# A planned attention and softplus MLP kernel: another block order, single ranks, a quartered end

## The chip, the core and the metric

The kernel runs on one core of a Trainium2 chip. The metric is the device time of one execution in microseconds; lower is better. An execution is followed by its engines: TensorE (PE), VectorE (DVE), ScalarE (ACT), GpSimd (POOL), and SyncE (SP), which issues all the DMAs.

## What is computed

The reference is an attention with a compressive memory, followed by a two-layer perceptron with softplus. The two weight matrices arrive as 64-bit words.

```python
B, H, S, D = 4, 8, 576, 64
scores = causal(q @ k.T / sqrt(D))
local = softmax(scores) @ v
q_p = elu(q) + 1
mem_out = (q_p @ M_prev) / (q_p @ z_prev + 1e-6)
x = sigmoid(beta) * mem_out + (1 - sigmoid(beta)) * local      # 2304 tokens x 512
out = softplus(x @ w_in) @ w_out                               # w_in 512 x 2048, w_out 2048 x 512
```

## The kernel before

**Blocks.** Each of the four batches is cut into two windows of queries, A (256 tokens) and B (320), so there are eight token blocks, numbered 0 to 7: even ones are A (narrow), odd ones B (wide). A batch has four pairs of heads (16 units of V in all), and a pair in a window is a "half", 0 to 31. The 2048 hidden columns are 16 groups f of 128.

**Three kinds of work.** (1) Attention: for each half `memory`, `chunks`, `values` make 128 rows of x and write them, as a high and a low part, to `xhl` and to DRAM (`xd`). (2) Fill: when the four halves of a block are done, `fill` multiplies x by the groups f = 0 to 6 (`hin`, then products into `part` in DRAM). Their weights are decoded at the start from 64-bit words (`decode`: load, one step on POOL or ACT, three on DVE, then a high and a low half; the low half of the pairs in `PELO` is made by two PE matmuls and an ACT copy, that of the others by a POOL subtraction). (3) Tail: `rest`, for each block in `ORDER`, reloads x, scales it (`halved`, with a square on ACT at L1011, a POOL clamp, a PE sum and small DVE steps), runs the groups f = 7 to 15 in float16 high and low parts, and adds `part`. Their weights come from `second`: load into a ring of two buffers (`ws` for w_in, `ws2` for w_out), decode, a square on ACT (L522), POOL clamp (L503), PE sum (L493), scale on DVE, then the two halves on ACT and DVE. `group` needs the scales of all 18 weights, and the g of every tail block (`parts16`, L1120 and L1122) needs `group`. `OPT['zp']` says which of these weights (number 2f + i, i = 1 for w_out) have their first step on ACT (L363) and not on POOL (L359).

**Plain and halved blocks.** A tail block in `SEVEN` computes x @ w_in for pairs of groups with seven products of half the columns in place of eight (`seven`, L1170; `combos` makes sums of the weights, on POOL for the pairs in `OPT['sp']`, their low halves on POOL for `OPT['sl']`; `halved` adds x's parts at L1015, on POOL for blocks in `OPT['zx']`). The other two blocks are `plain` (L394). The out-products are L1285; they collect in PSUM, and at a block's end DVE adds `part` (L1297) and SP sends the output (L1299).

**What sets the order.** Every operation is put on record by `op(engine, duration, rank, fn, reads, writes, dma=...)`. `Plan.run` then goes through time with these durations and gives each engine, of the operations that could start within 60 ns of the earliest, the one with the lowest rank. The order that results is fixed per engine: the engine's queue runs in that order, and an operation that waits holds all behind it. Ranks come from tables: `DEC` for `decode`, `SLOT` and `RK` for attention, `DT` for `second`, `XT` and `RKT` for the tail. A DMA's landing is reckoned as 1.4 us, its `dma` time behind the queue, and 0.7 us. Where PE is expected to idle in the first 130 us, filler matmuls (L1383) are put in. At the start 40 matmuls (L1375) run as warm-up.

**Buffers.** `xhl` has two buffers, used in the order of the calls: fill 6 and fill 7 hold them last in attention, the first tail block takes that of fill 6. The pools of the late weights and of the tail (`wl`, `wr`) open when attention's pools are released. For halves under `PHS` the feature map of `memory` stays in two parts and PE sums them (L911); for the others POOL adds them first (L903).

**V's scale.** `v_prep` finds a power of two for V of a unit. For units in `OPT['ab']` it is DVE's absolute maximum (L855); for the others two ACT passes of Relu (L847) with an added sum (L860).

**The end.** In `rest` each group's out-product has two parts of two 128-row quarters, and each part has its eviction and its output DMA. The last block is number 2, narrow.

Of the kernel before, what the change touches and what calls it, by code (L numbers as in the profile page):

```python
# [13 lines left out]
BF16 = mybir.dt.bfloat16  # L14
# [17 lines left out]
ORDER = [7, 0, 3, 4, 5, 1, 6, 2]  # L32
SEVEN = {1, 2, 3, 4, 5, 6}
CAP = 320
DEC = {(0, 0): -482.398, (1, 0): 24.68, (2, 0): -334.061, (3, 0): -530.087, (4, 0): -67.263, (5, 0): -115.974, (6, 0): 76.265, (0, 1): -777.236, (1, 1): 776.884, (2, 1): 980.305, (3, 1): 576.745, (4, 1): 532.208, (5, 1): -1374.13, (6, 1): -320.298}
PELO = {(0, 1), (4, 0), (2, 1), (1, 1), (2, 0), (5, 1), (3, 0), (1, 0), (4, 1)}
PHS = 12
RK = {'v': -14.703, 'mem': 77.969, 'prod': 27.412, 'norm': 41.42, 'r': -75.809, 'hi': -54.159, 'lo': 49.423, 'vhi': -231.603, 'vlo': 9.162, 'val': -74.716, 'qz': -35.724}
SLOT = {0: -523.489, 3: 179.471, 20: -126.975, 2: -551.32, 24: -61.418, 8: -436.367, 17: -51.528, 13: -174.167, 12: -191.109, 5: -136.439, 27: -23.647, 9: 273.018, 6: 31.405, 23: -191.858, 26: -120.491, 29: 70.495, 22: -62.923, 16: -216.806, 10: -1.497, 21: 29.964, 14: -303.101, 4: -317.571, 15: -59.449, 28: -418.019, 7: -98.43, 19: 320.22, 25: -47.394, 1: 14.992, 11: -79.481, 18: 247.429, 30: 186.958, 31: 184.083}
# [60 lines left out]
class Plan:  # L100
# [182 lines left out]
def attn_softplus_moe(  # L283
# [559 lines left out]
    def v_prep(u, k):  # L843
        va, vb, sc = u.va, u.vb, u.sc

        def acc(j):
            A.activation(out=vb()[:, 0].bitcast(BF16), in_=va(), func=AF.Relu, scale=1.0 - 2.0 * j,  # L847
                         accum_out=sc()[:, 3 + j:4 + j])

        def total():  # L850
            return sc()[:, 5:6].bitcast(BF16)[:, 0:1]

        sp = R["sm"].new()
        if u.no in OPT["ab"]:
# [14 lines left out]
        def scale():  # L869
            si = sc().bitcast(I32)  # L870
            V.tensor_scalar(out=si[:, 0:1], in0=sp().bitcast(I32)[:, 0:1], scalar1=0x7F800000, scalar2=None,
                            op0=ALU.bitwise_and)
            V.tensor_scalar(out=si[:, 1:2], in0=si[:, 0:1], scalar1=-1.0, scalar2=float(261 << 23), op0=ALU.mult,
                            op1=ALU.add)

        op("DVE", 340, k, scale, r=[sp], w=[(sc, 1)])
# [376 lines left out]
    LAG = 3  # L1253

    def rest(bi):
# [4 lines left out]
        for t in range(2):  # L1260
            op("SP", 450, 0, lambda t=t: SY.dma_start(out=xh()[:, t, :, :n], in_=xd[:, t, :, t0:t0 + n]),
               r=[(X[bi], p) for p in range(4)], w=[(xh, 4 * t + p) for p in range(4)], dma=5.8 * n)
# [4 lines left out]
           r=[(PART[bi], dm) for dm in range(4)], w=[(pp, e) for e in range(2)], dma=5.8 * n)  # L1267
# [8 lines left out]
        fs = [f for f in FINE]  # L1276
        for pair in PAIRS:
# [12 lines left out]
        for e in range(2):  # L1290
# [150 lines left out]
```

## Time and profile before

| | |
|---|---|
| time, median of 3 executions | 592.14 us (591.72 to 594.23) |
| the profiled execution | 597.28 us, of which span 595.5 us |
| granted clock of TensorE, mean | 0.993 of 2.4 GHz |
| PE busy | 567.5 us |
| DVE busy | 445.3 us |
| ACT busy | 376.1 us |
| POOL busy | 179.1 us |
| DMA | 90.11 MB, mean 151 GB/s |
| filler matmuls L1383 | 10.3 us of PE's busy time |

The span runs from the first to the last instruction; the profiled execution's own time is 1.8 us longer. Busy time of PE counts filler and warm-up too. Waits are put down to the instruction that released them, which may itself have waited; they have to be followed back.

### The profile page before, as it was taken

What the parts mean: (1) busy time and instruction counts of PE and PEld (TensorE: products, weight loads), DVE (VectorE), ACT (ScalarE), POOL (GpSimd) and SP (SyncE); (2) the same over time, 40 slices, a digit from 0 to 9 for tenths busy, and PEclk for the clock granted to TensorE, in tenths of its full rate; (3) what the DMA queues carried; (4) which work ended last, traced back from release to release, by engine and by line L of the source; (5) the groups of instructions that cost most, each with busy time, mean ns of one, the idle gap of its engine ahead of it and who ended that gap; (6) DMA issues with size and microseconds to landing.
All of it is one profiled execution on the core that took longest, in us unless ns stands there. A gap on an engine that the chain in (4) does not pass through costs nothing. (4 is left out here: it accounts for less than half of the span.)

```text
span 595.5 us, 14222 instructions
## 1 busy us (share of the span) xinstructions
PE 567.5 (95%) x5412; PEld 475.2 (80%) x5412; DVE 445.3 (75%) x1027; ACT 376.1 (63%) x1007; POOL 179.1 (30%) x265
## 2 busy tenths in 40 slices
PE   6989999899999999999999979989999999999996
PEld 5666667787887888788879979856888898888996
DVE  6698788888878789889885759979776566665643
ACT  6656766656566675777563657765565566565653
POOL 3664432545437334445541100003600101000100
PEclk9999999999999999999999979999999999999999
DMA  8654458997899899999969753940231432221111
GB/s 305 211 175 138 166 157 211 202 204 163 181 215 197 203 175 190 199 140 203 175 139 195 257 177 127 309 147 0 90 126 36 140 110 80 72 81 36 47 36 36
DMA packets 131027, 90.11 MB, mean 151 GB/s; under 512 B 85904, under 2 KB 122768, under 8 KB 130960
## 3 DMA queue, kind: packets, MB, share of 16 engines
q1 hardware_dynamic: 130960, 89.22, 59.7%
q8 instruction: 42, 0.69, 0.5%
q14 instruction: 25, 0.20, 0.1%
HBM read 49.84 MB, written 18.87 MB: 115 GB/s over the span
## 5 line engine op out<-in xcount | busy, mean ns | idle before, releaser
L1285 PE MATMUL s<-g,y 128*128 128x320 f16 (+1 forms) x864 | 120.4, 286 | 1.2 <-ACT g L1120 0.8
L394 PE MATMUL h<-xhl,w 128*128 128x256 f32 (+1 forms) x672 | 102.4, 301 | 1.4 <-ACT gl L1221 1.1
L394 PE MATMUL h<-g,w 128*128 128x256 f32 (+1 forms) x672 | 101.7, 303 | 0.8 <-ACT gl L1221 0.3
L1285 PEld LDWEIGHTS <-y 128*128 128x128 f16 x864 | 81.7, 98 | 19.4 <-issue 1.7
L394 PEld LDWEIGHTS h<-xhl,w 128*128 128x128 f32 x672 | 91.8, 189 | 6.2 <-issue 1.9
L394 PEld LDWEIGHTS h<-g,w 128*128 128x128 f32 x672 | 92.6, 192 | 4.5 <-issue 2.0
L729 POOL TENSOR_SCALAR PHL<-P,rr 128x384 f16<-128x384 f32 (+3 forms) x100 | 62.7, 642 | 75.5 <-DVE rr L709 28.4
L679 ACT ACTIVATE P<-s,nm 128x128 f32<-128x128 f32 (+3 forms) x128 | 66.5, 526 | 3.7 <-DVE rr L707 0.9
L1122 DVE SCALAR_TENSOR_TENSOR g<-gq,iv,g 128x320 f16<-128x320 f32 (+1 forms) x72 | 41.1, 581 | 28.4 <-ACT g L1120 28.2
L733 DVE SCALAR_TENSOR_TENSOR PHL<-P,rr,PHL 128x384 f16<-128x384 f32 (+3 forms) x100 | 58.5, 608 | 0.2 <-POOL PHL L729 0.2
L668 DVE TENSOR_REDUCE nm<-s 128x2 f32<-128x768 f32 (+2 forms) x64 | 51.0, 816 | 9.3 <-PE s L662 9.1
L1120 ACT ACTIVATE g<-gq,iv 128x320 f16<-128x320 f32 (+1 forms) x72 | 37.5, 531 | 5.1 <-PE s L1285 2.2
L1170 PEld LDWEIGHTS <-w 128*128 128x128 f16 x576 | 39.1, 98 | 1.8 <-issue 0.3
L1187 ACT ACTIVATE gq<-gq,iv 128x320 f32<-128x320 f32 (+3 forms) x48 | 21.6, 468 | 29.7 <-DVE gq L1182 29.6
L394 PE MATMUL h<-x,v 128*128 128x320 f16 (+1 forms) x288 | 38.1, 286 | 2.0 <-ACT gq L1139 1.4
L1221 ACT ACTIVATE gl<-h 128x256 f32<-128x256 f32 (+1 forms) x56 | 22.8, 409 | 27.0 <-PE h L394 26.8
L503 POOL TENSOR_SCALAR xs<-xs 128x1 bf16<-128x1 f32 x8 | 6.8, 847 | 98.5 <-ACT x L1011 98.5
L394 PEld LDWEIGHTS <-v 128*128 128x128 f16 x288 | 27.8, 98 | 10.2 <-issue 3.3
L957 PEld LDWEIGHTS <-vb 128*64 128x64 f16 x508 | 25.3, 109 | 11.5 <-issue 7.2
L327 DVE TENSOR_TENSOR g<-gl,g 128x256 fp32r<-128x256 f32 (+1 forms) x56 | 28.0, 506 | 8.5 <-ACT g L333 7.5
L1170 PEld LDWEIGHTS <-v 128*128 128x128 f16 x432 | 30.3, 98 | 2.4
L674 ACT ACTIVATE nm<-nm 128x2 f32<-128x2 f32 (+2 forms) x64 | 12.9, 202 | 27.3 <-DVE nm L668 24.6
(190 smaller groups left out, 1094.0 us busy)
## 6 DMA issues: line engine op xcount, KB each, us to landing
ws<-in_w_in_dram SPq DMA_DIRECT2D x16, 512.0 KB, 4.5
ws<-in_w_out_dram SPq DMA_DIRECT2D x16, 512.0 KB, 4.3
va<-in_nat_dram SPq DMA_DIRECT2D x16, 320.0 KB, 4.8
xd<-xhl SPq DMA_DIRECT2D x16, 320.0 KB, 3.3
xhl<-xd SPq DMA_DIRECT2D x8, 640.0 KB, 6.4
kB<-in_nat_dram SPq DMA_DIRECT2D x16, 288.0 KB, 3.9
xd<-xhl SPq DMA_DIRECT2D x16, 256.0 KB, 3.1
xhl<-xd SPq DMA_DIRECT2D x8, 512.0 KB, 4.8
```

The costliest lines, as they stand in the source:

```text
L327: eng.tensor_tensor(out=out, in0=in0, in1=in1, op=ALU.subtract)
L394: MM(out, lhsT=l, rhs=r, start=start and i == 0, stop=stop and i == len(pairs) - 1)
L668: V.tensor_reduce(out=nm()[:, 2 * j * both:2 * j * both + 2], in_=s()[:, :, so[j]:so[j] + n], op=ALU.max, axis=AX.X, negate=True)
L679: A.activation(out=pt()[:, po[j] + h * n:po[j] + h * n + n], in_=s()[:, h, so[j]:so[j] + n], func=AF.Softplus, scale=SCALE, bias=nm()[:, o ...
L729: P.tensor_scalar(out=o[:, :, 0, h, :], in0=src, scalar1=rs, scalar2=0.0, op0=ALU.mult, op1=ALU.add)
L733: V.scalar_tensor_tensor(out=o[:, :, 1, h, :], in0=src, scalar=rs, in1=o[:, :, 0, h, :], op0=ALU.mult, op1=ALU.subtract)
L957: MM(out, lhsT=vb()[:, vi, kc, 64 * h:64 * h + 64], rhs=rhs, start=False, stop=(kc == kcs[-1] and i == len(combos) - 1), skip_group_check= ...
L1120: op("ACT", 200 + .833 * n, -1, lambda: A.activation(out=g()[:, 0, :n], in_=gl(), func=AF.Copy, scale=sc()), r=gr + [(iv, 1)], w=[(g, 0)])
L1122: op("DVE", 165 + 1.04 * n, -1, lambda: V.scalar_tensor_tensor(out=g()[:, 1, :n], in0=gl(), scalar=sc(), in1=g()[:, 0, :n], op0=ALU.mult, ...
L1170: MM(bank()[:, :m], lhsT=left(s, kd, u), rhs=right(q, kd, v), start=first and not kd and not z, stop=kd == 1 and z == 2, skip_group_check= ...
L1221: op("ACT", 170 + .833 * n, -1, lambda: A.activation(out=gl()[:, :n], in_=hp()[:, :n], func=AF.Softplus, scale=XSC), r=[hp], w=[gl])
L1285: MM(bank(dm), lhsT=l, rhs=r, start=f == fs[0] and q == 0 and (not small or dm % 2 == 0), stop=f == fs[-1] and q == 2, skip_group_check=True)
```

## The change

Eight things change together. `ORDER` begins with block 3 (now the plain wide one) and puts block 7, attention's last, fifth; `SEVEN` follows. A table `NUDGE` adds a rank to 243 single operations, counted in the order of the `op` calls. The tables of ranks and of engines get other values (`PELO` loses (4, 0) and (1, 0); `PHS` goes from 12 to 11). For units not in `OPT['ab']` (3 before, 3 and 9 after) the sum of squares of one ACT pass takes the place of the two Relu passes. The load of x in the tail is reckoned at 7.0 n in place of 5.8 n. The last block's out-product has three parts, quarters (0, 1), (2,) and (3,), each with its eviction and DMA, and the last one's rank is `END` = 3 later. From `NUDGE` the entries are left out.

```diff
-ORDER = [7, 0, 3, 4, 5, 1, 6, 2]
-SEVEN = {1, 2, 3, 4, 5, 6}
+END = 3.0
+NUDGE = {47: -426.683, 52: -428.4095, 65: 40.465,
...
+ORDER = [3, 0, 5, 1, 7, 6, 4, 2]
+SEVEN = {1, 2, 4, 5, 6, 7}
 CAP = 320
...
-PELO = {(0, 1), (4, 0), (2, 1), (1, 1), (2, 0), (5, 1), (3, 0), (1, 0), (4, 1)}
-PHS = 12
+PELO = {(0, 1), (2, 1), (1, 1), (2, 0), (5, 1), (3, 0), (4, 1)}
+PHS = 11
...
-OPT = {'rp': {0, 3, 6, 8, 9, 19, 22, 27, 29, 30, 31}, 'hp': {0, 1, 2, 3, 8, 11, 13, 14, 17, 19, 20, 21, 23, 24, 25, 27, 28, 31}, 'ev': {0, 6, 7, 8, 13, 14, 15, 17, 18, 19}, 'pf': -15.94638586787345, 'hold': 0.0, 'ab': {4, 5, 6, 7, 8, 9, 10, 11, 12, 13, 14, 15}, 'gp': {1, 2, 5}, 'two': {0, 1, 3, 4, 5, 6, 7, 8, 10, 11, 14, 15}, 'zp': {1, 4, 6, 8, 10, 11, 13, 14, 15, 16, 17, 18, 19, 20, 21, 23, 25, 27, 28, 29, 30, 31}, 'zx': {0, 2, 3, 7}, 'sp': {14}, 'sl': {10, 12, 14}}
-DT = {(6, 0): 434.702, (6, 1): 651.572, (7, 0): 449.356, (7, 1): 501.508, (8, 0): 522.299, (8, 1): 468.268, (10, 0): 564.182, (10, 1): 533.892, (12, 0): 513.681, (12, 1): 532.918, (14, 0): 480.203, (14, 1): 520.884}
-XT = {0: 526.321, 1: 506.125}
-RKT = {'g': 30.767, 'sw': 1174.478, 't': 438.336, 'x': 0.346}
+OPT = {'rp': {0, 3, 6, 8, 9, 11, 16, 19, 22, 25, 27, 30, 31}, 'hp': {1, 2, 3, 7, 8, 11, 13, 14, 24, 25, 28, 29, 31}, 'ev': {6, 7, 8, 13, 14, 17, 18, 22, 23}, 'pf': -17.201271111318714, 'hold': 0.0, 'ab': {4, 5, 6, 7, 8, 10, 11, 12, 13, 14, 15}, 'gp': {1, 2}, 'two': {0, 1, 3, 4, 5, 6, 7, 10, 11, 13, 15}, 'zp': {2, 4, 5, 8, 9, 10, 14, 15, 16, 17, 18, 19, 20, 21, 23, 26, 27, 28, 29, 30}, 'zx': {0, 2, 4, 5, 7}, 'sp': {8, 14}, 'sl': {12, 14}}
+DT = {(6, 0): 647.49, (6, 1): 388.272, (7, 0): 583.883, (7, 1): 507.609, (8, 0): 508.843, (8, 1): 403.966, (10, 0): 587.939, (10, 1): 728.848, (12, 0): 537.814, (12, 1): 532.368, (14, 0): 478.779, (14, 1): 714.138}
+XT = {0: 539.253, 1: 862.136}
+RKT = {'g': 406.199, 'sw': 1239.132, 't': -51.211, 'x': -211.262}
...
+        o.rank += NUDGE.get(len(self.ops), 0.0)
...
-        def acc(j):
-            A.activation(out=vb()[:, 0].bitcast(BF16), in_=va(), func=AF.Relu, scale=1.0 - 2.0 * j,
-                         accum_out=sc()[:, 3 + j:4 + j])
+        top = u.no in OPT["ab"]
+
+        def acc():
+            A.activation(out=vb()[:, 0].bitcast(BF16), in_=va(), func=AF.Square, accum_out=sc()[:, 3:4])
...
-            for j in range(2):
-                op("ACT", 920, k, lambda j=j: acc(j), r=[va], w=[(vb, 0), (sc, 3 + j)])
-            op("DVE", 175, k, lambda: V.tensor_tensor(out=total(), in0=sc()[:, 3:4], in1=sc()[:, 4:5], op=ALU.add),
-               r=[(sc, 3), (sc, 4)], w=[(sc, 5)], port=True)
+            op("ACT", 830, k, acc, r=[va], w=[(vb, 0), (sc, 3)])
+            op("POOL", 150, k, lambda: P.tensor_scalar(out=total(), in0=sc()[:, 3:4], scalar1=2.0 ** 120, scalar2=2.0 ** -120,
+                                                       op0=ALU.min, op1=ALU.max), r=[(sc, 3)], w=[(sc, 5)])
...
-               r=[(X[bi], p) for p in range(4)], w=[(xh, 4 * t + p) for p in range(4)], dma=5.8 * n)
+               r=[(X[bi], p) for p in range(4)], w=[(xh, 4 * t + p) for p in range(4)], dma=7.0 * n)
...
+        parts = [(0, 1), (2,), (3,)] if bi == ORDER[-1] else [(0, 1), (2, 3)]
+        first = []
...
-                for e in range(2):
-                    op("PE", 6 * (.417 * n + 2.5), k + i + LAG - .5, lambda out=out, e=e: out(e=e),
-                       r=[(g, 0), (g, 1), (V2[f], 0), (V2[f], 1)], w=[(acc[0 if small else e], e)], mode="x")
+                for e, dms in enumerate(parts):
+                    o = op("PE", 3 * len(dms) * (.417 * n + 2.5), k + i + LAG - .5 + (END if dms == (3,) else 0),
+                           lambda out=out, dms=dms: out(dms=dms),
+                           r=[(g, 0), (g, 1), (V2[f], 0), (V2[f], 1)], w=[(acc[0 if small or not e else 1], e)], mode="x")
+                    if f == fs[0]:
+                        o.preds.update(first[1:])
+                        first.append(o)
```

## Rows read from the trace of the kernel before

**Rows 1.** Windows, four stages: length, busy us (instructions), clock, DMA

```profile
0.00:130.00 130.00, 118.47 (x1046) 89.74 (x1047) 101.80 (x249) 86.38 (x260) 60.32 (x103) 1.00 0.69 196
130.00:320.00 190.00, 188.56 (x1806) 156.99 (x1806) 162.03 (x386) 122.62 (x372) 88.61 (x131) 1.00 0.91 183
320.00:405.00 85.00, 75.37 (x555) 67.99 (x554) 62.12 (x133) 55.96 (x122) 6.04 (x14) 0.96 0.63 196
405.00:596.00 191.00, 185.12 (x2010) 160.48 (x2008) 119.35 (x263) 111.13 (x255) 24.16 (x17) 0.99 0.22 69
```

**Rows 2.** Windows, the filler matmuls of line 1383 alone, first stage

```profile
0.00:130.00 130.00, 10.33 (x68) 8.62 (x68) 1.00 0.69 196
```

**Rows 3.** Timeline of PE, 339 to 353: start, us, work, [idle before <-releaser]

```profile
339.76 4.86 PE L394 MATMUL h<-g,w 128*128 128x256 f32 x39 [0.22 <-ACT pb L1248]
348.13 0.17 PE L493 MATMUL h<-wsb,mean 128*128 128x2 bf16 x1 [3.51 <-POOL wsb L503]
348.58 4.83 PE L394 MATMUL h<-g,w 128*128 128x256 f32 x21
```

**Rows 4.** Timeline of DVE and ACT, 342 to 348 us

```profile
342.60 0.69 DVE L374 SCALAR_TENSOR_TENSOR wu<-ws,wu 128x512 int32<-128x512 int32 x1
...
345.83 1.27 ACT L1011 ACTIVATE x<-xhl 128x1280 f16<-128x1280 f32 x1 [4.87 <-DMA xhl<-xd]
...
347.10 0.61 ACT L522 ACTIVATE ws<-wu 128x512 f32<-128x512 f32 x1
```

**Rows 5.** The chain of waits, 329 to 346 us: start, length, what

```profile
329.15 7.93 PE h L394 x65
337.08 8.73 DMA xhl<-xd
```

**Rows 6.** Windows, the stretch behind the wait of 344 us

```profile
348.20:353.50 5.30, 5.05 (x25) 4.99 (x26) 4.64 (x11) 3.37 (x6) 0.00 (x0) 0.50 0.53 154
```

**Rows 7.** Timeline of SP's DMA issues: attention's last output

```profile
328.14 0.52 SPq L991 DMA_DIRECT2D xd<-xhl  x1
```

**Rows 8.** Timeline of ACT and PE, 389 to 391 us

```profile
389.15 0.66 ACT L363 ACTIVATE wu<-ws 128x512 f32<-128x512 f32 x1 [2.36 <-DMA ws<-in_w_out_dram]
...
390.28 1.79 PE L394 MATMUL h<-x,v 128*128 128x320 f16 x12 [1.42 <-ACT gq L1139]
```

**Rows 9.** Timeline of PE at 16 us; by form: POOL subtraction, PE feature sum

```profile
16.03 1.03 PE L566 MATMUL h<-wu,ident 128*128 128x512 f32 x2
...
17.13 0.39 PE L651 MATMUL s<-mask,identb 128*128 128x256 bf16 x2
...
L327 POOL TENSOR_TENSOR w<-wu,w 128x512 fp32r<-128x512 f32 x5 | 6.4, 1282 | 3.3 <-ACT w L333 3.1
...
L911 PE MATMUL sm<-qA,pe 128*128 128x130 f32 x32 | 6.2, 275 | 0.0
```

**Rows 10.** Timeline of the end, PE and DVE

```profile
586.65 4.09 PE L1285 MATMUL s<-g,y 128*128 128x256 f16 x36
...
590.78 1.41 DVE L1297 SCALAR_TENSOR_TENSOR pp<-s,xs,pp 128x512 f32<-128x512 f32 x2 [2.21 <-PE s L1285]
```

**Rows 11.** Timeline of DVE and POOL from 409; window 420 to 440

```profile
408.95 0.42 DVE L327 TENSOR_TENSOR w<-w 128x256 f32<-128x256 f32 x1
...
420.91 5.41 DVE L327 TENSOR_TENSOR w<-w 128x256 f32<-128x256 f32 x3
...
422.62 3.09 POOL L1015 TENSOR_TENSOR xhl<-xhl 128x1280 f32<-128x1280 f32 x1
...
420.00:440.00 20.00, 20.00 (x191) 17.76 (x190) 16.39 (x27) 11.63 (x19) 7.63 (x4) 1.00 0.24 69
```

**Rows 12.** DMA issues: KB each, median us to landing

```profile
out_dram<-pp SPq DMA_DIRECT2D x8, 256.0 KB, 2.2
```

**Rows 13.** Timeline of PE, the last two scale matmuls

```profile
392.89 0.16 PE L493 MATMUL h<-wsb,mean 128*128 128x2 bf16 x1 [0.82 <-POOL wsb L503]
...
400.57 0.18 PE L493 MATMUL h<-wsb,mean 128*128 128x2 bf16 x1
```

More of the change, by code (lines that the diff above doesn't have):

```diff
@@ L39 @@
-SLOT = {0: -523.489, 3: 179.471, 20: -126.975, 2: -551.32, 24: -61.418, 8: -436.367, 17: -51.528, 13: -174.167, 12: -191.109, 5: -136.439, 27: -23.647, 9: 273.018, 6: 31.405, 23: -191.858, 26: -120.491, 29: 70.495, 22: -62.923, 16: -216.806, 10: -1.497, 21: 29.964, 14: -303.101, 4: -317.571, 15: -59.449, 28: -418.019, 7: -98.43, 19: 320.22, 25: -47.394, 1: 14.992, 11: -79.481, 18: 247.429, 30: 186.958, 31: 184.083}
+DEC = {(0, 0): -337.459, (1, 0): 25.287, (2, 0): -1718.437, (3, 0): -684.042, (4, 0): 128.15, (5, 0): -71.362, (6, 0): 695.756, (0, 1): -302.323, (1, 1): 959.525, (2, 1): 895.79, (3, 1): 688.279, (4, 1): 526.761, (5, 1): 167.44, (6, 1): -386.313}
@@ L870, in scale @@
             si = sc().bitcast(I32)
[L871 to L876, printed above, removed]
+            if top:
+                V.tensor_scalar(out=si[:, 0:1], in0=sp().bitcast(I32)[:, 0:1], scalar1=0x7F800000, scalar2=None,
+                                op0=ALU.bitwise_and)
+                V.tensor_scalar(out=si[:, 1:2], in0=si[:, 0:1], scalar1=-1.0, scalar2=float(261 << 23), op0=ALU.mult,
+                                op1=ALU.add)
+                return
+            V.tensor_scalar(out=si[:, 6:7], in0=sp().bitcast(I32)[:, 0:1], scalar1=1, scalar2=0x7F800000,
+                            op0=ALU.logical_shift_right, op1=ALU.bitwise_and)
+            V.tensor_scalar(out=si[:, 1:2], in0=si[:, 6:7], scalar1=-1.0, scalar2=float(197 << 23), op0=ALU.mult, op1=ALU.add)
+            V.tensor_scalar(out=si[:, 0:1], in0=si[:, 6:7], scalar1=1.0, scalar2=float(64 << 23), op0=ALU.mult, op1=ALU.add)
+        op("DVE", 340 if top else 450, k, scale, r=[sp], w=[(sc, 1)])
         op("ACT", 830, k + RK["vhi"], lambda: A.activation(out=vb()[:, 0], in_=va(), func=AF.Copy, scale=sc()[:, 1:2]),
@@ L1266, in rest @@
         op("SP", 450, 0, lambda: SY.dma_start(out=pp()[:, :, :n], in_=part[:, :, t0:t0 + n]),
-           r=[(PART[bi], dm) for dm in range(4)], w=[(pp, e) for e in range(2)], dma=5.8 * n)
+           r=[(PART[bi], dm) for dm in range(4)], w=[(pp, e) for e in range(3)], dma=5.8 * n)
         small = n <= 256
@@ L1281, in rest, with out @@
             for i, f, g in zip(range(i0, NF * 99), pair, gs):
-                def out(f=f, g=g, e=0):
-                    for dm in (2 * e, 2 * e + 1):
+                def out(f=f, g=g, dms=()):
+                    for dm in dms:
                         for q, (l, r) in enumerate(out_pairs(f, g(), dm, n)):
@@ L1286, in out, with evict @@
                                stop=f == fs[-1] and q == 2, skip_group_check=True)
-                for e in range(2):
-                    op("PE", 6 * (.417 * n + 2.5), k + i + LAG - .5, lambda out=out, e=e: out(e=e),
-                       r=[(g, 0), (g, 1), (V2[f], 0), (V2[f], 1)], w=[(acc[0 if small else e], e)], mode="x")
-        for e in range(2):
-            a = acc[0 if small else e]
-            def evict(e=e):
-                o = pp()[:, 2 * e:2 * e + 2, :n]
-                src = (acc[0]().rearrange("p a (d n) -> p (a d) n", n=256)[:, 2 * e:2 * e + 2, :n] if small
-                       else acc[e]()[:, :, :n])
+                for e, dms in enumerate(parts):
[5 more added lines that the diff above has]
+                        first.append(o)
+        for e, dms in enumerate(parts):
+            a = acc[0 if small or not e else 1]
+            d0, d1 = dms[0], dms[-1] + 1
+            def evict(d0=d0, d1=d1):
+                o = pp()[:, d0:d1, :n]
+                src = (acc[0]().rearrange("p a (d n) -> p (a d) n", n=256)[:, d0:d1, :n] if small
+                       else acc[d0 // 2]()[:, d0 % 2:d0 % 2 + d1 - d0, :n])
                 V.scalar_tensor_tensor(out=o, in0=src, scalar=xs()[:, 4:5], in1=o, op0=ALU.mult, op1=ALU.add)
-            op("DVE", 150 + 2.1 * n, -1, evict, r=[(a, e), (xs, 5)], w=[(pp, e)])
-            op("SP", 450, 0, lambda e=e: SY.dma_start(
-                out=outT.rearrange("(d p) n -> p d n", p=128)[:, 2 * e:2 * e + 2, t0:t0 + n],
-                in_=pp()[:, 2 * e:2 * e + 2, :n]), r=[(pp, e)], dma=2.9 * n)
+            op("DVE", 150 + 1.05 * n * (d1 - d0), -1, evict, r=[(a, e), (xs, 5)], w=[(pp, e)])
+            op("SP", 450, 0, lambda d0=d0, d1=d1: SY.dma_start(
+                out=outT.rearrange("(d p) n -> p d n", p=128)[:, d0:d1, t0:t0 + n],
+                in_=pp()[:, d0:d1, :n]), r=[(pp, e)], dma=1.45 * n * (d1 - d0))
     for (f, i), k in DEC.items():
```

12 lines of the change are left out of this document (7 added, 5 removed).

## The prediction

> **What bounds the kernel now.** I read the page's busy line first: TensorE (PE) is busy for 567.5 us, 95% of the span of 595.5 (the sum over the stages of [rows 1]). The profiled execution took 597.28 us, 5.1 us (0.9%) over the median of the shown runs, 592.14. I make the sum in the profiled execution's microseconds and subtract it from the median. A share of 95% says little alone, so the next view cuts the span into those four stages. From 130 to 320 us (attention beside the fill blocks) PE is idle for 1.4 of 190 us. From 405 us to PE's last matmul at 590.7 us it is busy for 185.1 of 185.7 us. In those two stages only work taken off PE can shorten anything. The other two have room: 11.5 us idle in 0 to 130, and 9.6 us in 320 to 405, where the granted clock is 0.96. The first has more room than its busy time shows, since 10.3 us of it are filler matmuls of L1383 [rows 2], so 21.8 us there are start-up, waiting or filler.
>
> In the third stage one wait stands out. PE runs out at 344.6 us and gets its next matmul at 348.13, after 3.51 us, "<-POOL wsb L503" [rows 3]. That releaser is only the last link. POOL's clamp waited for ACT's square of a weight (L522), and that square stood in ACT's queue behind L1011, the square of the first tail block's x, which waited 4.87 us for its DMA [rows 4]. The weight had left DVE at 343.29. The chain of waits shows the same: the load xhl<-xd lasts 8.73 us from 337.08 [rows 5]. The clock fell behind the wait: 0.50 granted, thus the 1.2 GHz level, from 348.2 to 353.5 us [rows 6]. In it 21 matmuls took 4.83 us (0.230 us each) where 39 of the same form took 4.86 us (0.125 each) just before [rows 3]: 21 x 0.105 = 2.2 us lost. So one misplaced instruction costs PE 3.5 + 2.2 = 5.7 us.
>
> **The change, part by part.**
>
> Order of the blocks. The old first block, 7, needs attention's last output; 3 does not. But that output was issued at 328.14, while the load of the first tail block left at 337.08, released in the chain by the end of fill 6's in-products, which frees the xhl buffer [rows 5, 7]. Block 3 needs the same buffer. The shapes are the same too: plain wide, plain narrow, then three wide and three narrow halved blocks (the old order mixed these six). Price: 0, covered by the buffer wait; bounds 0 and, if the load could leave when attention's last output does, some -5 us.
>
> The first x in ACT's queue. The planner now reckons 7.0 n ns instead of 5.8 n for each of the two x loads, 0.77 us more in all for n = 320, and the first block's rank rises from 526 to 539. By its rule (1.4 us, the transfers, 0.7 us) it looked for the data at 337.08 + 5.8 = 342.9, just ahead of the weight that was ready at 343.29; the chip showed 345.8. Now it looks for them at 343.7, so L1011 should fall behind that L522. Bounds: 0 (the stall stays) and -5.7. With the square at 343.3 the next weight load, which waits for its buffer, leaves 3.7 us earlier than now (347.10 + 0.61 becomes 344.0), so the chain of 18 weights gains 3.7 us and not 5.7; the rest would come back as waits before 405. I take -3.7.
>
> Late weights' first step. Weights 25 and 31 (f 12 and 15 of w_out) get their first step on POOL instead of ACT, weight 26 the reverse. At 389.15 ACT sat 2.36 us for such a load with L1139, the release of an h bank, queued behind it; PE waited 1.42 us for that L1139 at 390.28 [rows 8]. POOL is idle there (6.0 of 85 us busy) [rows 1]. I take -1.4; bounds 0 (another load stands there instead) and -1.4.
>
> Two weights fewer have their low half made by PE (PELO loses (4,0) and (1,0)). Each takes PE from 16.03 to 17.13 us, 1.10 us, and becomes a 1.28 us subtraction on POOL [rows 9]. These lie before 90 us, where PE is also waiting and filling, so not every microsecond removed is a microsecond won: I take half of 2.2, -1.1. Bounds -2.2 and +2.6 (both subtractions waited for).
>
> Half 11 no longer splits its feature sum: two matmuls of 128x130 fewer. A row gives 0.275 us of each including drain [rows 9]; with PE full around there I take -0.4, bounds 0 and -0.55. The sum goes to POOL.
>
> V's scale from squares concerns unit 3 and unit 9. Unit 3 loses one ACT pass over V, unit 9 loses DVE's maximum and gains an ACT pass; each gets a tiny POOL clamp, and DVE's scale one more tiny instruction. PE is not released by them in any wait of the page; price 0, covered by ACT's 376 and POOL's 179 busy us of 595 [rows 1]; if that cover is gone, about 1 us either way. The moves of casts between POOL and ACT (rp, hp, gp, ev) and of score order (two) are of equal length: 0.
>
> The end. Now PE ends at 586.65 + 4.09 = 590.74, and DVE, idle until then, evicts both halves in one row of 1.41 us before the last output can leave [rows 10]. With END = 3 the last quarter's final matmuls come behind those of the other three, so only an eviction of 128x256 is left behind PE. A 256-wide DVE sum takes 0.42 us [rows 11]; with something for the read of PSUM I take 0.5, thus 1.4 - 0.5 = -0.9. The output's size halves as well: 256 KB land in 2.2 us [rows 12], so the flight saves between 0 and 1.1; I take 0, since the much smaller size can also be all latency. The Trainium skill ("DMA: Bandwidth & Descriptors", section "Latency and other measured facts") has a fixed cost of about 2 us per DMA, mostly the receipt from memory; by it next to nothing of the 2.2 us goes. The third output DMA on SP and its issue fall beside the last quarter's matmuls. Bounds 0 and -2.0.
>
> Ranks of single operations (NUDGE, 243 of about 3,000 operations, and new SLOT, RK, DEC, DT). By my count of the calls 5 fall on the decoding of the first weights, 117 on attention and fills, 17 on the later weights and combinations, 104 on the tail's blocks. In the two full stages they can win 1.4 + 0.6 us. In the first stage nothing shows what they do; nearest rows: -10 (half of its 21.8 us) and +6.0 (a new stall like that at 344, rounded up). I take 0.
>
> Sum: 3.7 + 1.4 + 1.1 + 0.4 + 0.9 = 7.5 us. 592.1 - 7.5 = 584.6.
>
> **The rivals.**
>
> (a) The early stage gives too. 5 to 6 us of its waiting and filler go, the PELO edits count in full: 578. That is 584.6 - 5.5 - 1.1. For it: 21.8 us are there, and the filler stands where PE was expected to find nothing to do, which another order of the same work can mend. Against it: nothing in the diff takes microseconds of work off DVE, which is 78% busy there [rows 1].
>
> (b) A new wait takes the old one's place. All 18 weights pass through two pairs of load buffers, and PE cannot start an out-product before the last scale. If L1011's move only lets PE arrive earlier at the same late weights, the two transition terms shrink from 5.1 to about 1 and the early 1.1 is eaten: 592.1 - 1.0 - 0.4 - 0.9 = 589.8. The 1.42 us at 390.28 [rows 8] speaks for it; that the weight's square was itself held by L1011 speaks against. That the planner still puts L1011 first (the change not doing what it says) ends here too.
>
> (c) POOL holds DVE in the tail. Pair 8's sums go to POOL and two more halved blocks get their 1280- or 1024-wide addition there; pair 10's low halves leave it. By the 3.09 us of one such addition that is some 9 us more and 2 less [rows 11]. Where POOL does such work now, DVE's sums stretch: three of 128x256 took 5.41 us instead of 3 x 0.42 while POOL added [rows 11]. At most one for one with POOL's time: 7 us more cost DVE between 0 and 7. PE does not feel it now, for DVE has 3.6 idle us of 20 there [rows 11]. If 7 come in front of the third block's g, all of it beyond that slack stops PE and brings the low clock: 3.4 + 2.2 + some waits behind, about 7, so 592. It decides from 3.6 us of DVE delay in that stretch on. The Trainium skill ("SBUF — State Buffer", section "SBUF: two separate sides") states it as a rule: the port pair that DVE and GpSimd share is an exclusive lock, held for a whole instruction against a DVE operation with two SBUF inputs. The trace agrees, with those 5.41 us.
>
> (d) Slower: the last weights come a turn later. The out-products wait for all 18 scales; the last two scale matmuls of PE stand at 392.89 and 400.57, one pair's turn of 7.7 us apart [rows 13]. The due ranks of the w_out pairs (14,1) and (10,1) rise from 521 to 714 and from 534 to 729, past the first x. If that costs one turn, PE, which has run out of in-products, stands for 7.7 us and resumes at the low clock, 2.2; the two transition terms don't come, for their place is this one: 592.1 - 1.1 - 0.4 - 0.9 + 7.7 + 2.2 = 599.6. For it: POOL, ACT and DVE have to take these weights beside the x work, which then goes first. Against: a rank decides only between operations that are ready together, and here each waits for its load first. It decides when the last scale comes over 3 us after 400.57.
>
> **How the numbers follow.** Forecast (581 to 589) 0.46; (a) 0.24; (b) 0.12; (c) 0.07; (d) 0.11. A measurement of this kernel can tell about 0.5%, 3.0 us, from no change: faster means under 589.2. So faster 0.70, same 0.19, slower 0.11. The range runs from 576 (the unpriced ranks at their better half) to 593 (over (b) and (c)), leaving out (d) and the far end of (a), about 0.2.
>
> **What would show it.** Right: no PE wait over 2 us and no clock of 0.50 between 320 and 405; L522 ahead of the first L1011 on ACT; seven L567 instead of nine; one eviction of 128x256 behind PE's last matmul, the output leaving about 0.5 us after it; PE still full from the first out-product on. Wrong: the first out-product still near 405 us (then (b)); PE waits on "DVE g L1122" with POOL busy beside it (then (c)); the last scale matmul later than 403 us (then (d)); PE idle and filler of 0 to 130 down by over 4 us (then (a)).

## The result and the profile after

The changed kernel took 586.4 us (median of 9 executions, 584.9 to 591.0), the kernel before in the same measurement 593.5 (591.7 to 595.6): a ratio of 0.9895, interval [0.9863, 0.9926], thus 6.2 us less, between 4.4 and 8.1. (The ratio is that of the means, 587.3 and 593.6; the medians lie 7.1 us apart. Differences below go by such ratios, unless medians are named.) A second measurement, beside the experiments below, gave 0.9906 [0.987, 0.9942]. The prediction was 584.6, faster. The time is right; the reason given for its largest term is not.

The profiled execution of the changed kernel took 590.98 us, span 589.2, granted clock 1.000 (before: 597.28, 595.5, 0.993). Lines have shifted by 3 to 17: L394 is now L397, L493 L496, L503 L506, L522 L525, L1011 L1021, L1261 L1271, L1285 L1297, L1297 L1314, L1383 L1400. The four stages of [rows 1] again, in the windows of the changed kernel (columns as there; the last stage ends 6 us earlier):

```profile
0.00:130.00 130.00, 118.75 (x1043) 91.69 (x1045) 101.85 (x243) 84.76 (x256) 67.47 (x108) 1.00 0.62 188
130.00:320.00 190.00, 186.47 (x1805) 155.31 (x1800) 160.09 (x391) 126.40 (x382) 82.92 (x126) 1.00 0.94 191
320.00:405.00 85.00, 80.88 (x618) 71.24 (x617) 66.13 (x136) 59.46 (x129) 14.31 (x22) 1.00 0.61 192
405.00:590.00 185.00, 178.52 (x1957) 155.10 (x1954) 108.74 (x252) 104.49 (x245) 25.46 (x18) 1.00 0.23 70
```

The third stage changed: PE works there 80.9 of 85 us, at full clock, where it worked 75.4 at 0.96. The early stages did not gain. The fillers of the first grew from 10.33 us [rows 2] to 11.88, and in the second PE idles 3.5 us in place of 1.4, all of it for one kind of transfer, five times, as the waits of PE from 130 to 320 us show (total, times, longest):

```profile
PE xp L967 <- DMA PTB<-PHL: 3.5, 5, 1.7
```

Where the stall of [rows 3] stood, PE's timeline of the changed kernel has this:

```profile
337.18 7.26 PE L397 MATMUL h<-g,w 128*128 128x256 f32 x60
344.44 0.16 PE L496 MATMUL h<-xs,mean 128*128 128x1 bf16 x1
345.05 0.16 PE L496 MATMUL h<-wsb,mean 128*128 128x2 bf16 x1 [0.45 <-DVE xs L504]
345.36 2.74 PE L397 MATMUL h<-g,w 128*128 128x256 f32 x21
```

The same 21 matmuls that took 4.83 us behind the stall take 2.74, and 0.45 us of waiting is left of 3.51. ScalarE's timeline tells how:

```profile
329.90 0.63 ACT L525 ACTIVATE ws<-wu 128x512 f32<-128x512 f32 x1
...
332.72 0.63 ACT L525 ACTIVATE ws<-wu 128x512 f32<-128x512 f32 x1
...
342.75 1.27 ACT L1021 ACTIVATE x<-xhl 128x1280 f16<-128x1280 f32 x1
...
344.02 0.61 ACT L525 ACTIVATE ws<-wu 128x512 f32<-128x512 f32 x1
```

The square of x (L1021) still stands **ahead** of the weight's square at 344.02, as in [rows 4]. It no longer waits: its data are there at 342.75. SP's queue before, and then of the changed kernel:

```profile
333.78 3.20 SPq L342 DMA_DIRECT2D ws<-in_w_in_dram  x2
337.08 2.04 SPq L1261 DMA_DIRECT2D xhl<-xd  x2
```

```profile
330.64 3.15 SPq L345 DMA_DIRECT2D ws<-in_w_in_dram  x2
337.38 0.94 SPq L1271 DMA_DIRECT2D xhl<-xd  x2
```

Both issue the two loads of x at 337, but before, a weight load of 512 KB left just ahead of them, at 336.65, and now the last one left some 3 us earlier. From issue to landing the x loads take 8.8 us before and 6.0 after (DMA issues between 325 and 350, last column):

```profile
xhl<-xd SPq DMA_DIRECT2D x2, 640.0 KB, 8.8
```

```profile
xhl<-xd SPq DMA_DIRECT2D x2, 640.0 KB, 6.0
```

The weight loads wait for a buffer that ScalarE's square (L522) frees. In the kernel before these squares ran at 333.03 and 335.91, behind four and six evictions of fill since attention's end; in the changed one at 329.90 and 332.72, behind two and four. Attention's end itself lay only 0.9 us earlier (table below). Issuing the x loads earlier was not open to the changed kernel: SP waited 3.5 us until PE's fill had freed their buffer, and issued them at 337.38.

The end, PE and DVE, then SP's issues:

```profile
578.77 3.11 PE L1297 MATMUL s<-g,y 128*128 128x256 f16 x27
582.73 1.14 PE L1297 MATMUL s<-g,y 128*128 128x256 f16 x9 [0.84 <-DVE pp L1314]
584.44 1.47 PE L1297 MATMUL s<-g,y 128*128 128x256 f16 x12 [0.58 <-DVE pp L1314]
...
585.95 0.48 DVE L1314 SCALAR_TENSOR_TENSOR pp<-s,xs,pp 128x256 f32<-128x256 f32 x1 [1.56 <-PE s L1297]
...
582.70 4.11 SPq L1316 DMA_DIRECT2D out_dram<-pp  x3
```

The last eviction is one of 128x256 and takes 0.48 us, as forecast. What [rows 10] did not have are two waits of PE for the evictions of earlier quarters. A third of this kind, 0.84 us for an eviction, stands at 429.92 in the changed kernel; in the kernel before PE waited only 0.17 us for evictions in this stage.

To add this up, each profile is cut at four events in PE's timeline: attention's last product with V (L957, now L967), fill's last product, the first and the last out-product. In us:

| profile | attention's end | to fill's end | to the first out-product | to the last | to the span's end |
|---|---|---|---|---|---|
| before | 327.0 | 53.7 | 24.1 | 185.9 | 4.7 |
| after | 326.1 | 48.5 | 24.1 | 187.2 | 3.3 |
| after, second profile | 323.3 | 48.2 | 25.7 | 187.2 | 3.3 |

Of the 6.3 us between the first two, 0.9 lie in attention, 5.2 in the stretch that held the stall, 1.5 at the end, and 1.3 are given back ahead of it. The changed kernel reaches attention's end with 336 of fill's matmuls still to do, before with 324. Attention's end is the weak column: five versions below that share the order of the kernel before up to there end at 322.7 to 324.9, and five profiles with the changed kernel's order at 323.3 to 328.1. So the profiles don't show attention to be faster.

### The profile page after: what moved, and what is told of

Its sections match the earlier page's. It is cut to its first block, busy times and chain, and to the rows that moved or that the text cites. A ratio compares the mean times of both kernels' runs of the same rounds, so it can differ in the third digit from the quotient of the medians.

```text
span 589.2 us, 14182 instructions
## 1 busy us (share of the span) xinstructions
PE 564.6 (96%) x5412; PEld 473.4 (80%) x5412; DVE 436.8 (74%) x1020; ACT 375.1 (64%) x1010; POOL 190.2 (32%) x273
## 4 chain that ended last, share of the span: by engine, by line
PE 78%; DMA 11%; DVE 6%; ACT 2%; issue 1%; SPq 1%; POOL 1%; ACTq 0%; POOLq 0%; DVEq 0%
PE h L397 28%; PE s L1297 17%; PE h L1180 6%; PE xp L967 5%; DMA PTB<-PHL 4%; DMA ws<-in_w_in_dram 4%; PE sm L921 3%; PE xp L1180 3%; PE s L620 3%; PE s L665 3%; DMA va<-in_nat_dram 2%; PE xp L981 1%; PE sm L1180 1%; PE xp L947 1%; PE s L598 1%; PE sm L1400 1%
## 5 line engine op out<-in xcount | busy, mean ns | idle before, releaser
L1297 PE MATMUL s<-g,y 128*128 128x320 f16 (+1 forms) x864 | 116.2, 286 | 3.0 <-DVE pp L1314 2.3
L397 PE MATMUL h<-xhl,w 128*128 128x256 f32 (+1 forms) x672 | 100.3, 300 | 0.5 <-ACT gl L1231 0.5
L1297 PEld LDWEIGHTS <-y 128*128 128x128 f16 x864 | 82.4, 98 | 22.2 <-issue 3.9
L397 PE MATMUL h<-g,w 128*128 128x256 f32 (+1 forms) x672 | 99.5, 299 | 0.2
L397 PEld LDWEIGHTS h<-xhl,w 128*128 128x128 f32 x672 | 90.9, 188 | 5.7 <-issue 3.1
L397 PEld LDWEIGHTS h<-g,w 128*128 128x128 f32 x672 | 90.6, 188 | 5.3 <-issue 3.8
L1132 DVE SCALAR_TENSOR_TENSOR g<-gq,iv,g 128x320 f16<-128x320 f32 (+1 forms) x72 | 39.0, 565 | 23.9 <-ACT g L1130 23.4
L397 PE MATMUL h<-x,v 128*128 128x320 f16 (+1 forms) x288 | 37.7, 286 | 1.5 <-DVE wsc L500 1.4
L967 PEld LDWEIGHTS <-vb 128*64 128x64 f16 x508 | 26.1, 109 | 14.8 <-issue 10.4
L397 PEld LDWEIGHTS <-v 128*128 128x128 f16 x288 | 27.8, 98 | 8.6 <-issue 1.7
L330 DVE TENSOR_TENSOR g<-gl,g 128x256 fp32r<-128x256 f32 (+1 forms) x56 | 26.5, 477 | 9.0 <-ACT g L336 8.0
L506 POOL TENSOR_SCALAR xs<-xs 128x1 bf16<-128x1 f32 x8 | 5.0, 624 | 75.9 <-ACT x L1021 74.4
```

The lines of the kernel that those rows point to most:

```text
L330: eng.tensor_tensor(out=out, in0=in0, in1=in1, op=ALU.subtract)
L397: MM(out, lhsT=l, rhs=r, start=start and i == 0, stop=stop and i == len(pairs) - 1)
L967: MM(out, lhsT=vb()[:, vi, kc, 64 * h:64 * h + 64], rhs=rhs, start=False, stop=(kc == kcs[-1] and i == len(combos) - 1), skip_group_check= ...
L1132: op("DVE", 165 + 1.04 * n, -1, lambda: V.scalar_tensor_tensor(out=g()[:, 1, :n], in0=gl(), scalar=sc(), in1=g()[:, 0, :n], op0=ALU.mult, ...
L1297: MM(bank(dm), lhsT=l, rhs=r, start=f == fs[0] and q == 0 and (not small or dm % 2 == 0), stop=f == fs[-1] and q == 2, skip_group_check=True)
```

## The experiments

All were timed in five rounds beside the kernel before; the interval is about 0.3% (1.8 us) either way, for the two halves of the tables 0.4 to 0.5%. The code is shortened to the lines that matter, for the halves of the tables to words.

**Half of the tables.** `tail_only` has the changed kernel's block order, late ranks, 7.0 n and quartered end, with attention's tables of before; `attn_only` has the opposite. Since one planner orders everything, each is a new plan.

```diff
-ORDER, SEVEN, DT, XT, RKT, OPT zp zx sp sl, rest(), NUDGE from 1886 on: of before
+the same: of the changed kernel          (tail_only; attn_only: the others)
```

> The kernel before with the tail's part of the change alone: order of blocks, ranks DT, XT, RKT and the single ranks from the first late weight on, engines zp, zx, sp, sl, the 7.0 n and the quartered end; attention's ranks and V's scale stay. Theory S (the gain is the wait of 344 us, and the tail's tables removed it): the first out-product comes 5 to 7 us earlier, no wait over 2 us between 320 and 405, and the time falls by 5 to 7 us. Rival A (the end of attention, 0.9 us earlier and with another queue on SP, removed the wait): the wait stays, the time moves by less than 2 us.

> The kernel before with attention's part of the change alone: DEC, PELO, PHS, RK, SLOT, the single ranks up to the first late weight, the engines of attention, V's scale; tail as before. Theory S: within 1.5 us of before, since in the changed kernel attention ends only 0.9 us earlier and with less of fill 6 done. Rival A: 5 to 7 us faster, the wait of 344 us gone. Forecast's term for the PE matmuls taken away: -1.5.

Measured: 600.1 us, ratio 1.0127 [1.0083, 1.0171], and 603.7, 1.016 [1.0106, 1.0214]. Neither half brings anything; they are 7.5 and 9.5 us slower than before, which neither theory nor rival had expected. In the profile of `tail_only` PE still waits for the weight's clamp, 3.3 us in all; in that of `attn_only` PE is busy for 181.46 us between 130 and 320, 7 less than in [rows 1]:

```profile
PE h L501 <- POOL wsb L511: 3.3, 2, 2.6
```

```profile
130.00:320.00 190.00, 181.46 (x1712) 148.09 (x1712) 157.24 (x384) 123.32 (x378) 85.22 (x128) 0.99 0.88 180
```

So the gain can't be divided between the tables, and the next versions keep a planned order and move single operations in it.

**The quartered end alone.**

```diff
-for e in range(2): ...                      # two parts
+parts = [(0, 1), (2,), (3,)] if bi == ORDER[-1] else [(0, 1), (2, 3)]
```

> The kernel before with the quartered last block alone. The forecast's term: -0.9 us. Theory W (the parts lie in one PSUM tile, and PE waits behind each eviction, as the changed kernel shows with 0.84 and 0.58 us): from PE's last block work on it gives back about 1.4 us of waits, so the net lies between -0.3 and +0.8 us.

Measured: 593.8 us, 1.0003 [0.9971, 1.0035], no gain. From PE's last matmul to the span's end its profile has 3.3 us where there were 4.7, but ahead of it the two waits:

```profile
586.51 0.81 PE L1288 MATMUL s<-g,y 128*128 128x256 f16 x6 [0.84 <-DVE pp L1305]
587.90 0.49 PE L1288 MATMUL s<-g,y 128*128 128x256 f16 x3 [0.58 <-DVE pp L1305]
```

**The forecast's move of L1011, on the kernel before.** First behind the next L522 on ScalarE; then behind that weight's clamp on POOL as well, with x's own clamp.

```diff
+order = behind(order, square, x)    # x_behind
+order = behind(order, clamp, x)     # x_behind2
```

> The kernel before with one instruction moved in the order that was planned: the square of the first tail block's x (L1011) goes behind the weight's square (L522) that stood next after it on ACT, with what hangs on it; nothing else changes. If the wait of 344 us is that one placement, PE's idle 3.5 us and the low clock behind it go, and the time falls by 3.7 us (forecast's term) to 5.7 (stall and clock). Rival B (PE only arrives earlier at the same late weights): the waits before 405 us grow by as much, and the time falls by less than 1.5 us.

> The kernel before at its own fixed order, with the copy of the tail's first x (L1011) moved behind ScalarE's square and GpSimd's clamp of the weight that the next fill needs, and x's own clamp behind that as well. Theory of the prediction (the stall at 344 is a matter of who stands first in ScalarE's and GpSimd's queues): the weight's whole chain no longer waits for the x load, the idle time at 344 falls from 3.5 to under 1 us, the granted clock stays at 1.0 behind it, and the time falls by 3 to 6 us. Rival (the x is needed next anyway, or another wait ends last there): less than 1.5 us, with PE idle of more than 2 us elsewhere between 338 and 353.

Measured: 593.3 us, 1.0009 [0.9979, 1.004], and 592.6, 0.9979 [0.9949, 1.0009]. In the first PE still waits 2.47 us for the weight's clamp, which POOL runs behind the clamp of x, at 342.58. In the second the weight's chain runs first and the wait comes back one link on, for x itself:

```profile
344.62 0.16 PE L493 MATMUL h<-xs,mean 128*128 128x1 bf16 x1 [2.80 <-POOL xs L503]
345.56 4.85 PE L394 MATMUL h<-g,w 128*128 128x256 f32 x21 [0.78 <-ACT pb L1248]
```

PE's queue has x's scale matmul right behind the weight's, and the 21 matmuls take 4.85 us, as long as at the low clock of [rows 3]. The rival of this run held: whichever of the two goes first, the x is late.

**The loads of x ahead of the weight load.**

```diff
+order = behind(order, loads[1], weight)   # on SP
```

> The kernel before at its own fixed order, with the weight load that SP issues just ahead of the first two x loads moved behind them. Theory that the x load was late because it shares the DMA with a weight load: x lands 2 to 4 us earlier, ScalarE's wait for it (4.87 us in the kernel before) falls to under 2 us, the stall at 344 shrinks to about 1 us, and the time falls by 2 to 5 us. Rival (the DMA is not what makes it late, or the weight that was moved is missed in turn): the wait stays or moves to the weight's square, and the time stays within 1.5 us or rises.

Measured: 597.5 us, 1.0058 [1.0033, 1.0082], slower. The x loads, issued at 334.72, released ScalarE at 340.12, after 5.4 us in place of 8.7; but now the weight load, issued at 336.64 behind them, takes 8.2 us and PE waits 6.09 for that:

```profile
344.82 0.64 POOL L359 TENSOR_SCALAR wu<-ws 128x512 f32<-128x512 f32 x1 [9.09 <-DMA ws<-in_w_in_dram]
...
348.45 0.17 PE L493 MATMUL h<-wsb,mean 128*128 128x2 bf16 x1 [6.09 <-POOL wsb L503]
```

Here the load that went second was late, as x was before, and both are needed. What is left to try is an earlier issue of the weight load.

**The weight loads earlier.** The two squares that free the buffers move ahead of fill's evictions on ScalarE; nothing else.

```diff
+order.remove(o); order.insert(max(order.index(p) for p in o.preds) + 1, o)   # two L522
```

> The kernel before at its own fixed order, with the two squares (L522) that free the weight buffers for SP's loads at 333.8 and 336.7 moved ahead of fill's evictions on ScalarE, right behind the decode that they wait for. Theory (in the kernel before the x load is late because SP is held by a weight load whose buffer the square frees late; the changed kernel has these squares 2 to 3 us earlier): SP issues the weight loads and the x loads 1 to 2.5 us earlier, the stall at 344 shrinks by as much, and the time falls by 1 to 4 us, more where the granted clock stays at 1.0. Rival (the x load is bound by the DMA queue or by its own buffer, whichever way the weights come, or fill's evictions are missed in turn): within 1 us of the kernel before, or slower.

Measured: 592.4 us, 0.9972 [0.9946, 0.9998]. The squares ran at 329.86 and 333.31, 3.2 and 2.6 us earlier; 2.0 us of that is attention's end, which came at 324.9 in this profile. The second weight load now left 2.4 us ahead of x (334.07 and 336.45), not 0.4, and the x that L1011 needs landed after 4.5 us. The profile shows the theory link by link, on ScalarE, PE and SP:

```profile
341.00 1.28 ACT L1011 ACTIVATE x<-xhl 128x1280 f16<-128x1280 f32 x1
...
343.93 0.18 PE L493 MATMUL h<-wsb,mean 128*128 128x2 bf16 x1
344.38 0.16 PE L493 MATMUL h<-xs,mean 128*128 128x1 bf16 x1 [0.27 <-DVE wsc L497]
344.60 2.75 PE L394 MATMUL h<-g,w 128*128 128x256 f32 x21
...
330.61 3.79 SPq L342 DMA_DIRECT2D ws<-in_w_in_dram  x2
336.45 0.94 SPq L1261 DMA_DIRECT2D xhl<-xd  x2
```

L1011 waits for no load, 0.27 us are left of the stall, the clock is 1.0. Moving two instructions of 0.63 us did it. The time fell by 1.7 us, 0.1 to 3.2: at the lower end of the 1 to 4 expected, for fill's evictions are now missed in turn (PE waits 2.4 us for L1221, before 1.4). At a mean clock of 0.998 or more, which 8 of its 12 executions had, it is no faster: they average 592.0 us, the 8 of 32 of the kernel before in this measurement 591.3. Its gain thus lies in how seldom the clock falls.

**The opposite, on the changed kernel.** The loads of x move behind the next weight load.

```diff
+order = behind(order, weight, loads[1])   # on SP
+order = behind(order, weight, loads[0])
```

> The changed kernel at its own fixed order, with the two first x loads issued behind the next weight load. If the gain of the change is the stall at 344 that it no longer has, this brings the stall back: ScalarE waits 3 us or more for the x load, PE is idle for 2 us or more there, the clock falls, and the time rises by 3 to 8 us above the changed kernel. Rival (the gain comes from the rest of the plan: fill ends earlier, fewer waits elsewhere): within 1.5 us of the changed kernel.

Measured: 595.0 us, 1.0013 [0.9989, 1.0037]; against 0.9895 of the changed kernel that is 7.0 us lost, all that the change had gained. The stall is back, and so is the low clock (21 matmuls in 4.33 us):

```profile
351.05 0.16 PE L496 MATMUL h<-xs,mean 128*128 128x1 bf16 x1 [4.63 <-POOL xs L506]
351.66 0.16 PE L496 MATMUL h<-wsb,mean 128*128 128x2 bf16 x1 [0.45 <-DVE xs L504]
351.68 4.33 PE L397 MATMUL h<-g,w 128*128 128x256 f32 x21
```

This stall is longer than that of before, since SP held the x loads until 344.26, and the profile has two more low stretches of the clock, from 177.5 and from 399.5 us; its price is an upper bound for the old one.

**The last quarter in its own PSUM tile.** On the changed kernel; the first two evictions are issued behind the third part's matmuls.

```diff
-acc = [R["s"].new() for _ in range(1 if small else 2)]
+acc = [R["s"].new() for _ in range(1 if small and not own else 2)]   # own: the last block
```

> The changed kernel with the last quarter of the last block's product in a PSUM tile of its own, and the evictions of the first two parts issued behind the third part's last matmul. Theory (the quartered end gave nothing because TensorE waits 0.84 and 0.58 us for evictions from the tile that all quarters share): these two waits go, and the time falls by 1.0 to 1.7 us below the changed kernel. Rival (the end is set by the last eviction and its output load, whichever way the quarters lie): within 0.5 us of the changed kernel.

> The changed kernel again, beside the versions that are built on it, on the same chip. Expected: a ratio of 0.986 to 0.993 to the kernel before, the granted clock at 1.0 between 338 and 355, no idle time of TensorE above 1 us there, and the two waits of 0.84 and 0.58 us behind the evictions at the end.

> The changed kernel with the last quarter in a PSUM tile of its own, again, to be set beside the changed kernel on the same chip. Theory from its first profile (the last matmul ran 1.7 us earlier against the last matmul of V's product, 8.73 against 10.43 us to the end of the span): 1.0 to 1.7 us below the changed kernel's median. Rival (what was gained at the end is lost in what varies from run to run, or in an earlier wait): within 0.5 us of it.

Measured: 587.6 us twice, ratios 0.989 [0.9863, 0.9917] and 0.9911 [0.9877, 0.9946]; the changed kernel beside the second, 588.4, 0.9906. In the profile the waits are gone, and PE runs through:

```profile
577.77 5.40 PE L1300 MATMUL s<-g,y 128*128 128x256 f16 x48
...
583.22 0.48 DVE L1317 SCALAR_TENSOR_TENSOR pp<-s,xs,pp 128x256 f32<-128x256 f32 x1 [0.49 <-PE s L1300]
```

From the start of the last row of out-products (577.77, in the changed kernel 578.77) to the span's end it is 8.7 us where the changed kernel needs 10.4, the 1.7 expected. The medians don't show it. One can see why: at a clock of 1.000 its executions average 585.6 us (5 of 18) and those of the changed kernel 587.3 (14 of 18), but it ran at that clock more seldom. Its low stretches in the profiles lie at 177 to 181 and at 39 to 46 us, where the order of its instructions is that of the changed kernel. Why they came more often is open, and so is whether this version is better: it is not shown to beat the changed kernel.

**PELO's rule.** The seven low halves left on PE go to POOL, on top of the version just shown; PE keeps a two-column matmul for each, and ScalarE a two-column copy.

```diff
-MM(d(), lhsT=ident, rhs=src()[:, 0:512], ...); MM(d(), lhsT=nident, rhs=wpart(f, i, 0), ...)
+MM(d()[:, 0:2], ...); sub(P, wpart(f, i, 1), src()[:, 0:512], wpart(f, i, 0))
```

> The kernel with the last quarter in its own tile, at its fixed order, and none of the seven low halves that TensorE still subtracts left on it: GpSimd does them in TensorE's place (about 1.28 us each), TensorE keeps a two-column matmul for each. Rule of the prediction (half of the time taken off a stage in which TensorE is busy for more than nine tenths comes out): seven times 1.03 us leave TensorE between 21 and 82 us, so 3 to 4 us less. Rival 1 (these seven lie in a stretch where TensorE already idles or runs fillers): within 1 us, with idle time in the place of the matmuls. Rival 2 (GpSimd's subtractions come later than TensorE's did, or hold VectorE): 1 us or more slower, with TensorE waiting for w or for VectorE in the first 130 us.

Measured: 589.5 us, 0.9945 [0.9912, 0.9977], by the medians 1.9 us above the version it is built on (587.6, 0.9911). The two intervals overlap, so that it is slower isn't clear of noise; the 3 to 4 us less of the rule are excluded. The executions at a clock of 1.000 average 588.0 us (4 of 12), without the change 585.6 (5 of 18). The first 130 us, with it and then without:

```profile
0.00:130.00 130.00, 113.84 (x1020) 89.63 (x1021) 101.44 (x240) 80.91 (x255) 77.65 (x115) 0.99 0.62 188
```

```profile
0.00:130.00 130.00, 118.99 (x1033) 92.80 (x1034) 99.59 (x241) 84.35 (x256) 68.72 (x108) 0.97 0.62 188
```

PE did 5 us less, POOL 9 us more, and attention ended at 328.3 in place of 325.4. PE now waits in that stretch for POOL's results, of which it waited for none without the change, and 2.8 us in one wait for DVE's xhl, where it was 1.3 in two:

```profile
PE s L834 <- POOL wu L363: 1.0, 1, 1.0
...
PE s L834 <- POOL w L331: 1.0, 1, 1.0
```

So what leaves PE early isn't won, and the waits are those of rival 2; that they cost more than the matmuls did is likely, not shown.

## Why the prediction was right, and where it was not

**First x in ACT's queue (-3.7).** The reading of the stall was right: it held PE, it brought the low clock, and 5.2 of the 6.3 us that the profile gained lie there. The step that failed is "L1011 should fall behind that L522". It did not, and the runs that made it do so were 0.5 us slower and 1.2 us faster, with intervals that hold 0. I had followed the chain of waits back to the load of x [rows 5] and stopped at its place in ScalarE's queue; one link further stands the weight load issued 0.4 us ahead of it, and behind that the square that had freed its buffer late. Where no weight load left in the 2 us ahead of x (`load_swap`, `squares_early`), the x that L1011 needs took 5.4 and 4.5 us in place of 8.7. `squares_early` shows that this is enough to remove the stall; on the changed kernel, `after_x_late` shows that the loads' times are what keeps it away. That the 0.4 us alone explain the 8.7 is not shown: in `after_x_late` a weight load also left 0.42 us ahead of x, and the first x landed after 5.1 us; there the next weight load left 7.1 us behind x (351.36), in the kernel before 3.9 us (340.99). By size the term was too large for the kernel before: 1.7 us [0.1, 3.2] alone.

**Late weights (-1.4).** Half right: PE's wait for the release of the h bank (L1139, now L1149) fell from 1.42 to 0.58 us, but the next wait, for a weight's scale at 389.85, is 1.39 long (rows below). The stretch from fill's end to the first out-product is 24.1 us in both profiles; only twelve more of the in-products are done by then (168 against 156), about 1.2 us of PE's busy time.

```profile
388.29 0.18 PE L496 MATMUL h<-wsb,mean 128*128 128x2 bf16 x1 [0.58 <-ACT gq L1149]
389.85 6.38 PE L397 MATMUL h<-x,v 128*128 128x320 f16 x54 [1.39 <-DVE wsc L500]
396.14 0.18 PE L496 MATMUL h<-wsb,mean 128*128 128x2 bf16 x1
...
398.70 0.30 PE L1297 MATMUL s<-g,y 128*128 128x320 f16 x1 [0.40 <-ACT g L1130]
```

**PELO and half 11 (-1.1, -0.4).** PE's matmuls went as said: 14 in place of 18 for the low halves, 28 in place of 32 for the feature sum (four fewer; I had counted two). The rule "half of what leaves PE" failed: `own_pelo0` gives +0.27 us for each low half moved (by the medians, not clear of 0), so these two cost about 0.5 if they behave like the seven, a value inside the bounds but on the other side. The profile's first two stages show no gain: 1.5 us more filler, 2.1 us more waiting.

**The end (-0.9).** The terms were right, 0.9 us less eviction and 0.5 us less from there to the end of the span (3.3 to 2.8), where I had taken 0 of between 0 and 1.1. The landing itself took 1.7 us for an output of 128 KB (the two in the DMA issues from 576 us on), where 256 KB took 2.2 [rows 12]. The Trainium skill ("DMA: Bandwidth & Descriptors", section "Latency and other measured facts") has a fixed cost of about 2 us per DMA; most of the 2.2 us did stay, as by that; 0.5 us went, more than the next to nothing that the forecast drew from it. What failed is what I left out: a quarter that shares its PSUM tile with others waits for their evictions, 0.84 + 0.58 = 1.42 us, as much as was won. `quarters` measured the sum: 0.2 us more, 1.9 either way.

**Block order, V's scale, NUDGE (0, 0, 0).** The buffer did hold the first x load, as reckoned for the order of the blocks: SP waited 3.5 us for fill's last use of it. V's scale is in none of PE's waits after. The ranks can't be priced alone: half of the tables costs 7.5 to 9.5 us where the whole gains 6. Of the 7.5 us of the sum, removing the stall alone bears out 1.7, the late weights some 1.2, and the end and the early terms nothing. That the forecast came within 2 us is for a large part luck.

**The rivals.** (a) fell: fillers and idle time of the first stage did not shrink. (b) fell: the first out-product starts at 398.70, not near 405, though the new wait of 1.39 us is of its kind. Its other condition, that the planner still puts L1011 first, came true, but not its price, for the x was there in time. (c) fell: POOL did get 9.6 us more from 320 us on, but 8.3 of them before 405 (14.31 against 6.04 of [rows 1]); from the first out-product on DVE is busy for 114.9 us (before 119.6), and PE's only wait for DVE's g is 0.29 us. (d) fell: the last scale matmul is at 396.14.

**What stays open.** The stall's removal alone gives 1.7 us, the end nothing, and the whole 5.6 to 6.2; putting a longer stall back costs 7.0. So the stall's share of the gain lies somewhere between 1.7 us and all of it. At a clock of 1.000 the kernel before averages 591.2 us (9 of its 83 executions beside the experiments, one of 3,171 us left out) and the changed one 587.3 (14 of 18). About 4 us thus show without any low clock, and in all six profiles with the stall the clock fell. Against `squares_early`, which has no stall either, the changed kernel's profile is 2.1 us shorter from attention's end on (263.1 to 265.2): 1.9 in fill, 1.5 at the end, less 1.3 ahead of it. By subtraction the other 2 us would lie in attention, but the profiles don't show them there: it ends at 323.3 to 328.1 us with the changed order (five profiles), at 322.7 to 327.0 with that of before (six). Their cause is open. The block order and the x loads' reckoned 7.0 n were not tried by themselves.

## What to carry to other kernels

When a load is the last link of a stall, look at what was issued just ahead of it and at what let that go: an early instruction that frees a load buffer can matter more than the order of those that wait. Test a queue's order by moving one instruction in the order that is there; exchanging half of a jointly planned set of tables tests another plan. Where an accumulation is split so that parts can leave early, look for waits of PE behind the first evictions: here they cost 1.42 us, what the tail had saved, and a PSUM tile of its own for the last part removed them in the profile, though no gain shows in the median.

## What was not expected of the hardware

Of the twelve profiles at the two planned orders, six have a stall of PE near 344, from 2.47 + 0.63 us to 6.09 us; behind each the granted clock fell to 0.50, the 1.2 GHz level, and in none of the six without a stall. But it also fell, for 3 to 7 us, at places that had no such wait and not in each execution of the same order. In the second profile of the changed kernel PE waited 0.52 and 1.39 us near 386, and the clock there was 0.76; in the first one it waited 0.58 and 1.39 us at the same place of the order and kept 1.00 (windows from 385 to 392, second profile and then first):

```profile
385.00:392.00 7.00, 5.48 (x32) 3.74 (x33) 4.31 (x9) 2.84 (x8) 0.94 (x1) 0.76 0.06 21
```

```profile
385.00:392.00 7.00, 5.03 (x38) 3.48 (x37) 5.95 (x12) 3.16 (x9) 2.25 (x2) 1.00 0.29 95
```

So these idle times alone don't settle whether the clock falls; what does is open. A term for it, like my 2.2 us, is paid in some executions only: all but one of the 83 of the kernel before have a mean clock between 0.984 and 1.000 and take 599.2 to 588.7 us.
